# Decode attention on one core: where the first tile's value products stand in the TensorE queue

## Chip, cores, metric

The kernel runs on one core of one Trainium2 chip. The metric is device time in microseconds (us), the median of several executions. One execution of each kernel was also recorded by the profiler; all profile lines below come from such recordings, and their times count from the start of the span. On one core, a run more than 1.5% above the fastest of the same kernel counts as slow.

Some terms: tile *s* (0 to 7) is one step of the attention, eight heads of one batch row. *K0* to *K7* and *V0* to *V7* are the key and value tiles of the steps, 8.39 MB each. A tile has landed when the last of the sixteen landings that the trace records for its load has come. The granted clock is the share of TensorE's full clock that it was given in a stretch of time; TensorE is called warm at 1.00 and cold when it is clearly below.

## The reference, cut to what matters

```python
# A: attention of one query position over a cache; B=2, 32 heads, Sk=4096, Dh=128, D=512
q = (x @ wq).reshape(B, 1, 32, 128).transpose(0, 2, 1, 3)
p = softmax(einsum("bhqd,bhkd->bhqk", q, k_cache) * 128 ** -0.5)
a = einsum("bhqk,bhkd->bhqd", p, v_cache).transpose(...).reshape(B, 1, 4096) @ wo
# B: a small MLP, relu(x @ w1) @ w2;  g = sigmoid((x * gate_w).sum(-1))
return g * a + (1 - g) * b
```

There is one query per head, so every byte of K and V is read once: 134 of the 145 MB that are loaded.

## The kernel before

K has two buffers and V has one, 64 KB per partition each. The V buffer also holds the small weights at the start.

```python
kpool = ctx.enter_context(tc.tile_pool(name="kpool", bufs=2))
vpool = ctx.enter_context(tc.tile_pool(name="vpool", bufs=1))
# ... cut: PSUM pools, small tiles
```

The scores of a tile are made in four blocks. VectorE multiplies a block by the query in place (`mult`). TensorE adds up the products along the head dimension, with an identity matrix as weights (`red`); for block 1 it has no work, since VectorE adds that one up itself. VectorE then finishes the block (`scores`). The value products (`pv`, 64 matmuls) of a tile run during the next tile's step.

```python
for s in range(NS):
    if s >= 1: sums_mm(s - 1)
    mult(s, 0)                       # VectorE, needs K of tile s
    if s >= 2: evac(s - 2)
    if s >= 1: expand(s - 1)         # VectorE: probabilities for pv(s-1)
    red(s, 0)                        # TensorE
    if s == 0: mlp_h(); mlp_o()      # the MLP, TensorE (and a memset of hT on VectorE)
    # ... cut: comb, unpack, sums_inv of earlier tiles
    mult(s, 1)
    scores(s, 0)
    red(s, 1)                        # no TensorE work (block 1 is summed by VectorE)
    mult(s, 2)
    scores(s, 1)                     # VectorE, 8.7 us
    red(s, 2)                        # TensorE, waits for mult(s, 2)
    mult(s, 3)
    scores(s, 2)
    if s >= 1:
        pv(s - 1)                    # TensorE, the last reader of V of tile s-1
    red(s, 3)
    scores(s, 3)
    probs(s)
    if s == 0: load_v(0)
    if s + 2 < NS:
        load_k(s + 2)                # waits until K of tile s is free
        load_v(s + 1)                # waits until pv(s), in the next step, has read V of tile s
# ... cut: loads of V7 (into a K buffer) and wo, end of the last tile, output projection with wo
```

All these loads are issued by one queue (SyncE's, `SPq` in the profile), in program order. Each engine takes its own instructions in program order too; in the trace below, tile 0's value products have all their inputs at 80.9 us and start at 96.84 us, behind the sums that stand before them.

The softmax here doesn't subtract the row's maximum and nothing guards it: scores larger than these inputs give would overflow.

## Time and profile before

| | |
|---|---|
| time, median of 6 (20 with later runs) | 356.62 us (357.11) |
| the profiled execution | 355.56 us, span 353.9 us |
| mean DMA rate over the span | 411 GB/s |
| VectorE busy, TensorE busy | 74%, 52% |

The page cuts the span into 40 slices of 8.85 us. This is its row for the rate at which the DMA engines moved data, in GB/s:

```profile
GB/s 341 489 356 423 486 474 363 467 430 407 357 237 467 370 468 454 378 474 452 380 467 452 385 459 454 393 444 467 394 437 467 400 432 452 422 393 432 378 390 69
```

Between the start and the end, only the twelfth slice (97 to 106 us), at 237 GB/s, falls far below the others. The same place in a table of stretches; the columns are the stretch, its length, the busy time of PE (TensorE), PEld (its weight loads), DVE (VectorE), ACT and POOL, then granted TensorE clock, DMA share, GB/s:

```profile
90.00:96.50 6.50, 5.96 (x15) 2.18 (x15) 6.50 (x2) 0.00 (x0) 0.00 (x0) 0.53 0.77 333
96.50:101.80 5.30, 3.98 (x66) 1.70 (x65) 5.30 (x2) 0.00 (x0) 0.00 (x0) 1.00 0.42 139
101.80:108.00 6.20, 4.53 (x15) 1.75 (x15) 2.22 (x2) 0.00 (x0) 0.00 (x0) 0.72 0.93 391
...
135.00:137.00 2.00, 0.98 (x20) 0.36 (x13) 2.00 (x2) 0.00 (x0) 0.00 (x0) 1.00 1.18 500
```

The rates of such short stretches scatter (some read over 500). So I find holes from the packets themselves: a hole is where packets of fewer than 12 of the 16 DMA engines are under way. By that measure there is one after the start, 96.5 to 101.9 us (dips of under 0.5 us are left out here and below).

What did the queue wait for? The timeline of the loads' issues (start, length, issuing queue, line, operation, destination and source):

```profile
100.53 0.33 SPq L104 DMA_DIRECT2D vt<-in_A_v_cache_dram  x1
108.55 0.33 SPq L104 DMA_DIRECT2D kt<-in_A_k_cache_dram  x1
136.02 0.33 SPq L104 DMA_DIRECT2D vt<-in_A_v_cache_dram  x1
145.63 0.33 SPq L104 DMA_DIRECT2D kt<-in_A_k_cache_dram  x1
173.34 0.33 SPq L104 DMA_DIRECT2D vt<-in_A_v_cache_dram  x1
```

The first of them loads V1 into the buffer of V0. The TensorE timeline of that step (in brackets the idle time before a group, and what ended it):

```profile
78.80 5.30 PE L219 MATMUL red<-kt,ident 128*128 128x512 bf16 x16 [3.34 <-DVE kt L210]
90.54 6.37 PE L219 MATMUL red<-kt,ident 128*128 128x512 bf16 x16 [6.44 <-DVE kt L210]
96.84 3.64 PE L276 MATMUL o_ps<-vt,PT_sb 128*32 128x512 bf16 x64
103.47 5.04 PE L219 MATMUL red<-kt,ident 128*128 128x512 bf16 x16 [2.99 <-DVE kt L210]
```

L276 is `pv`. It frees the buffer at 100.5 us and the issue follows at once. TensorE sat idle for 6.44 us before the sums ahead of `pv`, waiting for a VectorE product that `pv` does not need.

The chain of waits, followed back from the end; four of its pieces (start, length, what):

```profile
255.28 42.59 DMA kt<-in_A_k_cache_dram
...
297.89 4.43 DVE kt L210
...
329.04 4.92 PE red L219 x16
...
345.67 5.29 PE a_ps L354 x24
```

The K7 load sits in the chain from its issue to its landing at 297.9 us, so the end of the kernel is tied to how far the stream has come. The rest, from 297.9 to 353.9, is work of VectorE and TensorE: 56.0 us, called the tail below.

### The profile page before, as it was taken

To read this page: it belongs to the slowest core of one execution; us is meant where nothing else is said; L and a number is where in the kernel's file an instruction comes from. 1 tells how busy PE (TensorE), PEld (TensorE's weight loads), DVE (VectorE), ACT (ScalarE), POOL (GpSimd) and SP (SyncE) were. 2 spreads that over 40 slices of the span, in tenths; PEclk is the share of its full clock that TensorE was granted. 3 is DMA by queue.
4 is the path that set the end of the run, shared out by engine and by line. 5 is a ranking of instruction groups with operands and counts; after the bars stand their busy time and mean duration, and the time that the engine had idled before them with its cause. 6 is when DMAs were issued, how large, how long until landed. Compare 5 with 4: busy or idle time off the path is not lost.

```text
span 353.9 us, 2493 instructions
## 1 busy us (share of the span) xinstructions
PE 184.8 (52%) x1091; PEld 74.6 (21%) x1091; DVE 262.3 (74%) x151; ACT 7.5 (2%) x23; POOL 6.1 (2%) x16
## 2 busy tenths in 40 slices
PE   0410856345764465564566286619424654728586
PEld 0100422111221122121222032203111221203232
DVE  3003189769977999599949994999569984999451
ACT  1000000000000000000000000000000000000000
POOL 6000000000000000000000000000000000000000
PEclk9985676688688869886976788687968698658889
DMA  8989998999869899899899899999999999999991
GB/s 341 489 356 423 486 474 363 467 430 407 357 237 467 370 468 454 378 474 452 380 467 452 385 459 454 393 444 467 394 437 467 400 432 452 422 393 432 378 390 69
DMA packets 4051, 145.60 MB, mean 411 GB/s; under 512 B 453, under 2 KB 586, under 8 KB 970
## 3 DMA queue, kind: packets, MB, share of 16 engines
q1 hardware_dynamic: 4036, 145.46, 95.9%
q8 instruction: 8, 0.13, 0.1%
q14 instruction: 1, 0.01, 0.0%
q10 hardware_dynamic: 6, 0.00, 0.0%
HBM read 145.46 MB, written 0.00 MB: 411 GB/s over the span
## 4 chain that ended last, share of the span: by engine, by line
DVE 59%; DMA 21%; PE 14%; issue 5%; ACT 0%; SPq 0%; DVEq 0%; ACTq 0%
DVE kt L210 32%; DMA kt<-in_A_k_cache_dram 21%; DVE sc L231 19%; PE red L219 10%; DVE PT_sb L251 4%; PE a_ps L354 2%; PE o_ps L276 2%; DVE osb L289 2%; DVE OT_sb L316 0%; DVE osb L287 0%; DVE tmp L307 0%; DVE rsg L268 0%; PE comb L301 0%; ACT e L237 0%; DVE rsg L267 0%
## 5 line engine op out<-in xcount | busy, mean ns | idle before, releaser
L219 PE MATMUL red<-kt,ident 128*128 128x512 bf16 x384 | 129.4, 512 | 139.8 <-DVE kt L210 139.8
L210 DVE TENSOR_TENSOR kt<-kt,qb 128x8192 bf16<-128x8192 bf16 x32 | 141.4, 4417 | 35.8 <-DMA kt<-in_A_k_cache_dram 26.9
L219 PEld LDWEIGHTS <-ident 128*128 128x128 bf16 x384 | 48.2, 125 | 217.6 <-issue 185.7
L231 DVE TENSOR_REDUCE sc<-kt 128x64 f32<-128x8192 bf16 x8 | 69.4, 8678 | 0.0
L231 DVE TENSOR_REDUCE sc<-red 128x64 f32<-128x512 f32 x24 | 16.5, 686 | 36.4 <-PE red L219 36.4
L276 PE MATMUL o_ps<-vt,PT_sb 128*32 128x512 bf16 x448 | 25.5, 380 | 0.0
L251 DVE TENSOR_TENSOR PT_sb<-e,tmask 128x2048 bf16<-128x2048 bf16 x8 | 18.3, 2283 | 0.6 <-ACT e L237 0.6
L276 PEld LDWEIGHTS <-PT_sb 128*32 128x32 bf16 x512 | 13.3, 100 | 18.0 <-issue 4.5
L237 ACT ACTIVATE e<-sc 128x256 bf16<-128x256 f32 x8 | 3.3, 417 | 285.6 <-DVE sc L231 285.6
L289 DVE SCALAR_TENSOR_TENSOR osb<-o_ps,jmask,osb 128x128 f32<-128x128 f32 x24 | 8.4, 351 | 0.8
L257 PE MATMUL gs<-partials,heads 128*128 128x1 f32 x16 | 3.0, 259 | 11.1 <-ACT e L237 11.1
L195 PE MATMUL mm<-vt 128*32 128x512 bf16 x64 | 5.7, 514 | 4.3 <-DMA vt<-in_A_wq_dram 3.7
L354 PE MATMUL a_ps<-kt,OT_sb 128*2 128x512 bf16 x32 | 7.2, 379 | 0.0
L276 PE MATMUL o_ps<-kt,PT_sb 128*32 128x512 bf16 x64 | 5.5, 508 | 1.9 <-DVE PT_sb L251 1.9
L307 DVE SCALAR_TENSOR_TENSOR tmp<-comb,rsg,umask 128x128 f32<-128x128 f32 x8 | 2.8, 346 | 4.2 <-PE comb L301 4.2
L257 PEld LDWEIGHTS gs<-partials,heads 128*128 128x128 f32 x16 | 2.4, 188 | 15.0 <-ACT e L237 13.2
L159 PE MATMUL comb<-ident,vt 2*128 2x2 bf16 (+1 forms) x8 | 0.6, 173 | 7.8 <-DMA vt<-in_gate_w_dram 5.6
L354 PE MATMUL a_ps<-vt,hT 128*2 128x512 bf16 x11 | 3.9, 524 | 0.5 <-ACT hT L347 0.5
L437 DVE CAST res<-a_ps 2x256 bf16<-2x256 f32 x1 | 0.4, 412 | 4.6 <-PE a_ps L354 4.6
L195 PEld LDWEIGHTS <-vt 128*32 128x32 bf16 x64 | 2.2, 119 | 7.4 <-issue 6.9
L354 PEld LDWEIGHTS <-OT_sb 128*2 128x2 bf16 x32 | 2.6, 84 | 4.1
L132 POOL TENSOR_SCALAR_AFFINE_SELECT vt<-vt 32x512 f32<-32x512 f32 x4 | 3.4, 847 | 0.2
(40 smaller groups left out, 33.1 us busy)
## 6 DMA issues: line engine op xcount, KB each, us to landing
vt<-in_A_wq_dram SPq DMA_DIRECT2D x1, 4096.0 KB, 12.1
kt<-in_A_v_cache_dram SPq DMA_DIRECT2D x1, 4096.0 KB, 31.3
kt<-in_A_v_cache_dram SPq DMA_DIRECT2D x2, 2048.0 KB, 40.2
kt<-in_A_wo_dram SPq DMA_DIRECT2D x3, 1024.0 KB, 9.5
vt<-in_B_w_dram SPq DMA_DIRECT2D x1, 1376.0 KB, 33.8
vt<-in_B_w_dram SPq DMA_DIRECT2D x1, 1280.0 KB, 36.5
kt<-in_A_wo_dram SPq DMA_DIRECT2D x1, 512.0 KB, 12.3
kt<-in_A_wo_dram SPq DMA_DIRECT2D x2, 256.0 KB, 11.6
```

Source lines behind the costliest of these rows:

```text
L132: nc.gpsimd.affine_select(out=sel[k * CG : (k + 1) * CG].rearrange("p j (t a) -> p j t a", t=T), in_=sel[k * CG : (k + 1) * CG].rearrange( ...
L195: nc.tensor.matmul(ps[j * CG : (j + 1) * CG, :], lhsT=xbp[:, b, c, e, :], rhs=wq_v[:, c, 2 * j + e, :, :], start=(c == 0 and e == 0), stop ...
L210: nc.vector.tensor_tensor(out=kt, in0=kt, in1=q, op=ALU.mult)
L219: nc.tensor.matmul(ps, lhsT=ident, rhs=prod[:, :, j * RW : (j + 1) * RW], start=(j == 0), stop=(j == Dh // RW - 1),)
L231: nc.vector.reduce_sum(out=sc_t[s][:, u * CU : (u + 1) * CU], in_=red_t.pop((s, u)), axis=AX.X)
L237: nc.scalar.activation(out=e, in_=sc_t.pop(s), func=ACT.Exp, scale=inv_sqrt_dh, accum_out=partials[:, s : s + 1],)
L251: nc.vector.tensor_tensor(out=out_, in0=e.to_broadcast(shape), in1=m.to_broadcast(shape), op=ALU.mult)
L257: nc.tensor.matmul(rs_t[s], lhsT=heads.rearrange("p t a -> p (t a)"), rhs=partials[:, s : s + 1], start=True, stop=True,)
L276: nc.tensor.matmul(o_t[s][k * CG : (k + 1) * CG, :], lhsT=PT_sb[:, s % 2, q, :], rhs=v_t[s][:, q * JB : (q + 1) * JB, :], start=(q < NCG), ...
L289: nc.vector.scalar_tensor_tensor(out=osb, in0=o[:, j, :], scalar=jmask[:, j : j + 1], in1=osb, op0=ALU.mult, op1=ALU.add,)
L307: nc.vector.scalar_tensor_tensor(out=tmp, in0=ps, scalar=rs_t.pop(s), in1=umask.unsqueeze(1).to_broadcast([P, DR, DA]), op0=ALU.mult, op1= ...
L354: nc.tensor.matmul(a_ps, lhsT=lhsT, rhs=rhs, start=start, stop=stop)
```

## The change

The value products of tile 0 are to run behind one score block of tile 1 instead of three, so that the V buffer is free sooner. Nothing else moves.

```diff
         scores(s, 0)
+        if s == 1:
+            pv(0)
         red(s, 1)
         mult(s, 2)
         scores(s, 1)
         red(s, 2)
         mult(s, 3)
         scores(s, 2)
-        if s >= 1:
+        if s >= 2:
             pv(s - 1)
         red(s, 3)
```

## The prediction

> **What bounds the kernel now.** Two resources are nearly even. The K/V stream: from 102 to 346 us the DMA queues run without a hole, and one 8.39 MB tile takes 19.35 us (spacing of tiles in the trace's packets), 433 GB/s, 38.7 us for a K and V pair. The Trainium skill, "DMA: Bandwidth & Descriptors", section "Where 436 GB/s comes from", puts the port ceiling at 435 GB/s; this trace agrees. VectorE: one tile step takes 37.1 us (spacing of successive tiles' first products in the timeline). So after the start the stream is the longer one, by 1.6 us a step, and the chain of waits shows it late: a 42.6 us DMA piece ends with the landing of the eighth K tile at 297.9 us; VectorE waits for K at 259.2 (3.22 us) and 297.9 (1.52 us). The tail follows the stream: the last output weights land at 348.9, span end 353.9.
>
> **The hole.** The packets show one hole after the start: 96.5 to 101.9 us, 5.4 us (the page's slice at 97 to 106 us shows 237 GB/s). Next comes the second V tile, into the single V buffer, which the first value products still read; they ran 96.84 to 100.5 us because the in-order TensorE puts them behind the third block's column sums (90.54 to 96.9), which wait for a VectorE product. The load was issued at 100.53.
>
> **What the change does.** No work is added or removed; 64 matmuls (3.64 us) move ahead of that sum. Their inputs are early: expanded probabilities at 80.9 us, V landed at about 79.5, the sums of block 0 end at 84.1. So they run 84.1 to about 88 us, before the third block's product is ready (90.5): that sum is not delayed. The V load is issued near 88, before the third K tile has drained (96.5): hole gone, V1 5.4 us earlier.
>
> **How much survives.** The next V load is issued at 136.02 us after the second tile's value products, which VectorE paces, plus 1.34 us from issue to first packet = 137.4. Today its data starts at 140.8; the shortened stream would want 135.4. So a new hole of about 2 us opens there and the carried shift is 140.8 - 137.4 = 3.4 us. The next V load has more slack (174.7 against 179.5), so 3.4 carries on. VectorE allows as much: its wait of 3.22 us at the seventh tile vanishes, the eighth's stays 1 to 2 us.
>
> Against it: "TensorE: Matmul & The Clock Gate", Part 1, says the default state is throttled and activity releases it; the trace agrees (granted clock 0.5 after idle stretches, 1.0 during the value products). These no longer warm TensorE before the second tile's last sums (5.04 us today; the first tile's cold ones took 5.72), for which VectorE waits. I take off 0.7 us as an estimate: it delays VectorE and the 136 us issue. Net 2.7 us.
>
> **Prediction: 353.8 us (-0.8%), range 352.0 to 355.8.** Faster by over 2%: 0.03; within 2%: 0.95; slower by over 2%: 0.02.
>
> **Right if the profile shows:** tile 0's value products at 84 to 88 us; second V load issued near 88; no hole at 96 to 102; a hole of 1.5 to 3 us near 135 to 138; seventh K tile landing near 256.4, VectorE waiting under 1 us for it; eighth near 295.1; output weights landing 2 to 3.5 us earlier; last sums of tile 1 taking 5.5 to 6 us.
>
> **Wrong if:** V lands after 84 us and TensorE stalls with the sums behind it; clock history delays tile 1's value products, widening the new hole; the hole of before varies between runs, so 5.4 us is not typical; or the tail absorbs the gain. If no new hole opened, the gain would reach 4 us at most, because VectorE then binds.

## The result, and the profile after

The median is **354.65 us** (10 runs, 349.5 to 357.34) against 357.11 us (20 runs of the kernel before, 355.15 to 359.4). A ratio is the mean time of one kernel's fast runs over the other's in the same rounds, so it is not quite the ratio of those medians: 0.9878, 95% interval 0.984 to 0.9917. That counts as the same within 2%, but the gain is clear of noise. One caution: a single execution at 349.5 us makes five of the ten runs "slow" by the 1.5% rule. With all runs of both, the means are 354.43 and 357.36, a ratio of 0.9918. Two later sets on other chips gave 0.9902 and 0.9946.

| profiled execution | before | after |
|---|---|---|
| time, span (us) | 355.56, 353.9 | 351.2, 349.5 |
| hole in the stream (us) | 96.5 to 101.9 | 135.1 to 136.4 |
| K6, K7 landed (us) | 259.2, 297.9 | 256.1, 294.8 |
| from K7's first product to the end (us) | 56.0 | 54.7 |

The same row of the page:

```profile
GB/s 319 514 368 407 514 368 473 428 413 474 375 465 480 368 466 377 360 480 428 414 473 368 473 398 452 465 375 465 459 398 458 390 459 465 390 405 424 404 391 66
```

The slice at 237 GB/s is gone. The same stretches as before:

```profile
90.00:96.50 6.50, 3.49 (x16) 1.46 (x15) 6.50 (x1) 0.00 (x0) 0.00 (x0) 1.00 0.98 423
96.50:101.80 5.30, 0.00 (x0) 0.00 (x0) 5.30 (x2) 0.00 (x0) 0.00 (x0) 0.70 1.09 470
101.80:108.00 6.20, 4.90 (x16) 1.77 (x15) 1.81 (x3) 0.00 (x0) 0.00 (x0) 0.71 0.83 359
...
135.00:137.00 2.00, 0.10 (x4) 0.10 (x1) 2.00 (x2) 0.00 (x0) 0.00 (x0) 1.00 1.27 434
```

The stretch of the old hole carries 470 in place of 139 GB/s. The new hole near 135 us is too short to stand out in a 2 us stretch; the packets show it (no new 64 KB packet of a load starts between 134.6 and 136.1 us). The issues:

```profile
87.03 0.33 SPq L104 DMA_DIRECT2D vt<-in_A_v_cache_dram  x1
107.74 0.33 SPq L104 DMA_DIRECT2D kt<-in_A_k_cache_dram  x1
135.15 0.33 SPq L104 DMA_DIRECT2D vt<-in_A_v_cache_dram  x1
144.82 0.33 SPq L104 DMA_DIRECT2D kt<-in_A_k_cache_dram  x1
172.46 0.33 SPq L104 DMA_DIRECT2D vt<-in_A_v_cache_dram  x1
```

The V1 load comes 13.5 us earlier. The later issues, up to that of K7 (255.28 and 254.38 us), come only 0.8 to 0.9 us earlier, because VectorE paces them. Most of that lead, 0.7 us, is there at the K2 load already (73.72 before, 73.05 after), ahead of the changed place: in this execution the sums and the MLP of tile 0 ran at a higher granted clock (0.62 against 0.57 from 33 to 43 us). The TensorE timeline:

```profile
78.14 5.29 PE L219 MATMUL red<-kt,ident 128*128 128x512 bf16 x16 [3.34 <-DVE kt L210]
83.35 3.64 PE L276 MATMUL o_ps<-vt,PT_sb 128*32 128x512 bf16 x64
89.88 3.61 PE L219 MATMUL red<-kt,ident 128*128 128x512 bf16 x16 [2.89 <-DVE kt L210]
102.81 4.90 PE L219 MATMUL red<-kt,ident 128*128 128x512 bf16 x16 [9.32 <-DVE kt L210]
```

The products fill the idle time. The sums behind them are not delayed, and run warm, in 3.61 instead of 6.37 us, which nobody needed. The chain:

```profile
254.38 40.40 DMA kt<-in_A_k_cache_dram
...
294.81 4.42 DVE kt L210
...
325.95 3.63 PE red L219 x16
...
341.30 5.29 PE a_ps L354 x24
```

Of the 4.4 us between the two spans, 3.1 us come from the stream (297.89 to 294.81). The other 1.3 us come from the last sums of tile 7: 4.92 us before (granted clock 0.73), 3.63 us after (1.00), for the same 16 matmuls.

### The profile page after: what moved, and what is told of

The parts are those of the page before. It is cut to its first block, busy times and chain, and to the rows that moved or that the text cites. A ratio compares the mean times of both kernels' runs of the same rounds, so it can differ in the third digit from the quotient of the medians.

```text
span 349.5 us, 2493 instructions
## 1 busy us (share of the span) xinstructions
PE 179.6 (51%) x1091; PEld 73.0 (21%) x1091; DVE 262.1 (75%) x151; ACT 7.5 (2%) x23; POOL 6.1 (2%) x16
## 4 chain that ended last, share of the span: by engine, by line
DVE 60%; DMA 20%; PE 13%; issue 5%; ACT 0%; SPq 0%; DVEq 0%; ACTq 0%
DVE kt L210 33%; DMA kt<-in_A_k_cache_dram 20%; DVE sc L231 20%; PE red L219 10%; DVE PT_sb L251 4%; PE a_ps L354 2%; PE o_ps L276 2%; DVE osb L289 2%; DVE OT_sb L316 0%; DVE tmp L307 0%; DVE osb L287 0%; DVE rsg L268 0%; PE comb L301 0%; ACT e L237 0%; DVE rsg L267 0%
## 5 line engine op out<-in xcount | busy, mean ns | idle before, releaser
L219 PE MATMUL red<-kt,ident 128*128 128x512 bf16 x384 | 125.7, 499 | 140.4 <-DVE kt L210 140.4
L219 PEld LDWEIGHTS <-ident 128*128 128x128 bf16 x384 | 47.0, 122 | 215.9 <-issue 185.1
L301 PEld LDWEIGHTS comb<-osb,pick 128*128 128x128 f32 x16 | 2.9, 190 | 2.1 <-issue 1.3
```

Source lines behind the costliest of these rows:

```text
L219: nc.tensor.matmul(ps, lhsT=ident, rhs=prod[:, :, j * RW : (j + 1) * RW], start=(j == 0), stop=(j == Dh // RW - 1),)
L301: nc.tensor.matmul(comb_t[s], lhsT=pick, rhs=osb_t.pop(s), start=True, stop=True)
```

## The experiments

Theory A is the prediction's: the gain comes from the V buffer, which is free sooner, so that the hole closes. Theory B: it comes from TensorE's order and clock. Theory C, tested by the fourth run: the hole is not a cause at all.

| kernel (label) | median us, runs | before, same rounds | ratio (95% interval) | hole, us | K7's first product | tail, us |
|---|---|---|---|---|---|---|
| before, first profile | 357.11, 20 | | | 96.5–101.9 | 297.9 | 56.0 |
| changed, first profile | 354.65, 10 | 357.11 | 0.9878 (0.984–0.9917) | 135.1–136.4 | 294.8 | 54.7 |
| e1_after_again | 354.79, 6 | 357.44 | 0.9902 (0.9863–0.9941) | 135.2–137.5 | 295.0 | 58.7 |
| e2_decouple | 354.07, 6 | 357.44 | 0.9906 (0.9882–0.9929) | 135.1–138.0 | 295.5 | 56.2 |
| e3_held | 364.88, 6 | 357.44 | 1.0219 (1.0188–1.025) | 96.3–110.3 | 306.6 | 58.8 |
| e4_pool_memset | 350.35, 6 | 357.44 | 0.982 (0.9786–0.9853) | none | 295.0 | 56.1 |
| e5_two_early | 352.31, 6 | 357.81 | 0.9848 (0.982–0.9876) | 173.8–175.5 | 294.8 | 56.3 |
| e6_all_early | 355.9, 6 | 357.81 | 0.9956 (0.993–0.9983) | 328.8–334.5 | 296.4 | 57.7 |
| e7_after_pool | 351.41, 6 | 357.81 | 0.9821 (0.9793–0.9849) | none | 292.2 | 57.4 |
| e8_pool_again | 350.08, 4 | 357.81 | 0.9787 (0.9762–0.9811) | none | 292.3 | 56.1 |
| e9_after_pair | 355.1, 6 | 356.7 | 0.9946 (0.9919–0.9973) | 135.0–138.2 | 295.7 | 56.2 |
| e10_two_pair | 351.61, 6 | 356.7 | 0.9877 (0.9838–0.9915) | 173.8–175.6 | 294.4 | 54.7 |

Hole, first product and tail are from each kernel's profiled execution; dips of up to 2.6 us after 329 us, where the last V load ends and the output weights begin, are told only for e6. By the 2% rule e3, e4, e7 and e8 count as unclear and the others as the same; every interval is clear of 1. e1 to e4, e5 to e8 and e9 with e10 share a chip each.

### e1_after_again: the changed kernel once more

> The changed kernel once more, on the chip of the next three. Theory A (the V buffer: the second V load is issued earlier and the hole in the K/V stream closes): second V load issued at 86 to 89 us, no hole near 96 us, a smaller hole of 1 to 2.5 us near 135 us, the seventh and eighth K tiles land 2.5 to 3.5 us earlier than in the kernel before; time 2 to 4.5 us shorter. The 1.3 us that the profiled run won beyond that, in the last column sums of the last tile, may or may not come back: it is a matter of the granted clock. Theory B (the gain comes from the order and the clock on TensorE itself: the sums of block 2 no longer run cold, the start was 0.7 us quicker): same time, but the gain sits in shorter column sums.

The V1 load was issued at 88.15 us, the hole was at 135.2 to 137.5 us, and K6 and K7 landed 3.0 and 2.9 us earlier than in the kernel before. The stream's gain came back. The tail's did not: the last sums took 6.5 us (granted clock 0.54) and the span was 353.7 us, with K7 at nearly the same time as in the first profile. One piece of its chain, against 3.63 us in the first profile of the same kernel:

```profile
326.13 6.52 PE red L219 x16
```

So of the profiled 4.4 us, the 3.1 us in the stream are the change's: e1 did not have the early lead (K2 was issued at 73.98 us) and still won 2.9 us there. The other 1.3 us are a higher clock that the first execution happened to get.

### e2_decouple: the old order, but nobody holds the buffer

```diff
-                rhs=v_t[s][:, q * JB : (q + 1) * JB, :],
+                rhs=(
+                    k_t[1][:, (q % (NQ // 2)) * JB : (q % (NQ // 2) + 1) * JB, :]
+                    if s == 0
+                    else v_t[s][:, q * JB : (q + 1) * JB, :]
+                ),
```

This is an edit of the kernel before. It computes wrong values; the comparison with the reference does not notice one tile's share of the output.

> Order of the kernel before on every engine, but the first tile's value products read the first half of the second K tile, so that nobody reads the first V tile and its buffer is free at once (wrong values on purpose). Theory A: the second V load is issued near 80 us, when the first V tile has landed; no hole near 96 us; hole of 1 to 2.5 us near 135 us; time within 1 us of the changed kernel's on this chip, although TensorE still does the value products behind the third block's sums. Theory B: TensorE's order is that of before, so time within 1 us of the kernel before.

The V1 load was issued at 79.36 us while `pv` ran at 95.2 us, in the old place:

```profile
79.36 0.33 SPq L104 DMA_DIRECT2D vt<-in_A_v_cache_dram  x1
...
95.23 3.64 PE L276 MATMUL o_ps<-kt,PT_sb 128*32 128x512 bf16 x64
```

The hole near 96 us was gone; the one near 135 us was 2.9 us long, a little over the expected 1 to 2.5. The time was 354.07 us, 0.7 us from the changed kernel on the same chip and 3.4 us below the kernel before. The gain therefore does not need TensorE's new order. Theory B falls.

### e3_held: the new order, but one matmul still holds the buffer

```diff
         if s == 1:
-            pv(0)
+            pv(0, 0, NQ - 1)
...
         red(s, 3)
+        if s == 1:
+            pv(0, NQ - 1, NQ)
         scores(s, 3)
```

This is an edit of the changed kernel.

> The changed kernel with 63 of the 64 first value products in the new place and the last one behind the fourth block's sums, so that the V buffer is held until about 108 us. Theory A: second V load issued near 108 us, a hole from 96.5 to about 109.7 us, 13 us in place of 5.4; time about 8 us longer than the kernel before (6 to 9). Theory B: TensorE's order is the changed kernel's but for one matmul, so the time is the changed kernel's within 1 us.

The V1 load was issued at 109.19 us, and the hole lasted from 96.3 to 110.3 us, 14 us.

```profile
109.19 0.33 SPq L104 DMA_DIRECT2D vt<-in_A_v_cache_dram  x1
```

The time rose by 7.4 us over the kernel before (364.88 against 357.44) and by 10 over the changed kernel. A hole 8.6 us longer cost 8.7 us at K7's first product (306.6 against 297.9): in this part of the stream a lost microsecond is a lost microsecond at K7.

### e4_pool_memset: close the hole from the other side

```diff
         if FREM:
-            nc.vector.memset(hT[: P - FREM, :, FF:], 0.0)
+            nc.gpsimd.memset(hT[: P - FREM, :, FF:], 0.0)
```

This is an edit of the kernel before; the value products stay where they were. The memset is 0.06 us of VectorE work. But VectorE is in order, and the memset has to wait for the MLP on TensorE and ScalarE, so the next product of tile 0 waited too. In the profile of the kernel before, that wait reads as 8.89 us of "issue".

> The kernel before, value products where they were; only the small memset of hT moves from VectorE to GpSimd, so that VectorE does not sit 8.9 us at 36.7 to 45.6 us behind the MLP. Theory A: VectorE's whole timeline up to the seventh tile comes about 8.5 us earlier, the old order issues the second V load near 92 us, before the stream drains at 96.5, and the third near 127.5: no hole at either place. The stream is 5.4 us ahead and the time 4.5 to 6 us shorter than before, more than the changed kernel gains. Theory C (VectorE and stream are bound elsewhere, the hole is no cause): VectorE only waits longer for the seventh and eighth K tiles, time within 1 us of before.

VectorE made its first two products back to back (32.43 to 41.2 us). Here is the second product of the kernel before, then the two of this run, then this run's V1 issue:

```profile
45.63 4.42 DVE L210 TENSOR_TENSOR kt<-kt,qb 128x8192 bf16<-128x8192 bf16 x1 [8.89 <-issue]
...
32.43 8.76 DVE L210 TENSOR_TENSOR kt<-kt,qb 128x8192 bf16<-128x8192 bf16 x2 [22.58 <-DMA kt<-in_A_k_cache_dram]
...
94.47 0.33 SPq L104 DMA_DIRECT2D vt<-in_A_v_cache_dram  x1
```

V1 was issued at 94.47 us and V2 at 130.07 us, both before the stream ran dry. No hole was left (only a dip of 0.4 us at 96.7 us). The time fell by 7.1 us, more than the expected 4.5 to 6. Theory C falls: the old place of the value products does no harm once VectorE comes earlier. K7, however, landed only at 295.0 us; e8 takes this up.

### e5_two_early: move the second tile's products too

```diff
-        if s == 1:
-            pv(0)
+        if s in (1, 2):
+            pv(s - 1)
...
-        if s >= 2:
+        if s >= 3:
             pv(s - 1)
```

This and the next are edits of the changed kernel.

> The changed kernel with the second tile's value products moved too (behind one score block of the third tile). Theory A: second V tile lands near 118 us, its products run at about 118 to 122 us, third V load issued near 122.5 in place of 135 to 136; the remaining hole near 135 us is gone; the K tiles from the fifth on land 1 to 2.5 us earlier than in the changed kernel. VectorE is then the limit at the seventh tile, so the time is only 0.5 to 1.5 us below the changed kernel's (353.5 on the last chip). If the second hole did not cost anything, the K tiles land when they did and the time is the same within 0.5 us.

The hole near 135 us went away (V2 issued at 123.5 us) and a third one opened at 173.8 to 175.5 us, where the next products, in the old place, hold the buffer until the V3 load at 174.37 us. I had expected the lead to last for the rest of the stream; it lasted one K tile. K4 landed 2.1 us earlier than in the first profile of the changed kernel, K7 at the same 294.8 us. The time was nevertheless shorter (see e10). (The "353.5 on the last chip" of the expectation is not a measured time: the changed kernel's median there was 354.79 us.)

### e6_all_early: move all of them

```diff
-        if s == 1:
-            pv(0)
+        if s >= 1:
+            pv(s - 1)
...
-        if s >= 2:
-            pv(s - 1)
```

> Every tile's value products behind one score block. Theory A: no hole anywhere, as in the run with two; from the fifth tile on the V tile lands only just before or after the sums of block 0 end, so TensorE waits up to 2 us for it, with 3 us or more to spare before VectorE needs the sums of block 2. Time that of the run with two moved, within 1 us. A rival, that value products early in the step hold up the sums, would make it 2 us or more slower.

Half a miss. The stream had no hole up to K7, which landed at 292.2 us, 5.7 us earlier than in the kernel before. But the time was 355.9 us, 3.6 us above the run with two. VectorE started K7 only at 296.43 us and did not wait for it: it had become the limit. Here is its wait for the fourth block's sums in tiles 5 and 6, in this kernel and then in the kernel before (VectorE timeline):

```profile
258.30 0.69 DVE L231 TENSOR_REDUCE sc<-red 128x64 f32<-128x512 f32 x1 [5.21 <-PE red L219]
...
295.82 0.69 DVE L231 TENSOR_REDUCE sc<-red 128x64 f32<-128x512 f32 x1 [5.24 <-PE red L219]
```

```profile
255.29 0.69 DVE L231 TENSOR_REDUCE sc<-red 128x64 f32<-128x512 f32 x1 [3.10 <-PE red L219]
...
295.68 0.69 DVE L231 TENSOR_REDUCE sc<-red 128x64 f32<-128x512 f32 x1 [4.79 <-PE red L219]
```

Over tiles 2 to 6 these waits add up to 25.6 us, against 22.3 us before: 3.3 us more. In the old place, `pv` runs just before those sums; in the new one, TensorE has been idle. The granted clock over the sums of tiles 5 and 6 was 0.62 in both here, against 1.00 and 0.68 before, and the same 16 matmuls took 5.72 and 5.75 us, against 3.61 and 5.30. So a lower clock goes with the longer waits; that the idle time caused it is not shown, since no run varied the clock alone. The expectation named a rival, value products that hold up the sums behind them, and its number (2 us or more slower) came true. But VectorE never waited for the sums right behind them, those of the third block; it waited for the fourth block's. TensorE itself waited longer for V tiles than expected (4.0 us in tile 6, up to 2 expected), which cost VectorE nothing.

### e7_after_pool and e8_pool_again: do the two gains add?

e7 is the changed kernel with e4's one-line edit; e8 is e4's kernel again, on e7's chip.

> The changed kernel with the small memset of hT on GpSimd instead of VectorE. Theory A: with VectorE 8 us earlier the old order had no hole left (none was in the run with that memset alone), so moving the value products adds nothing on top: the time is that of the memset alone within 1 us (350.4 on the last chip). If the two gains had different causes they would add, and the time would be near 347.5.

> The memset alone once more, as the partner of the run before on the same chip: 350 us, 6 to 7 us below the kernel before, no hole at 96 or 135 us. Its first profile showed the eighth K tile at 295.0 us, no earlier than in the changed kernel, although the first of the 16 landings came 2.4 us earlier than there; if that lag of the last landing was a matter of that one execution, this profile shows the tile at 292 to 294 us.

They do not add: 351.41 and 350.08 us, with ratios of 0.9821 and 0.9787 whose intervals overlap, and K7's first product at 292.2 us in e7 and 292.3 in e8. The 1.3 us between the medians are a little over the expected 1 us, and e7 is the slower one, far from the 347.5 us of gains that add. K7 landed at 292.2 us in e6, e7 and e8 alike, 5.7 us earlier than in the kernel before: that is what a stream without a hole gives here, however the hole is closed. In e8 the V1 load was issued at 91.93 us. Its K7 landed at 292.2 us, where e4's profile had 295.0. In e4's execution the sixteen landings of each late load were spread over some 4.1 us, against 1.9 us in e8's; the work waits for the last of them. What put part of the DMA engines behind in that execution stays open.

### e9_after_pair and e10_two_pair: the changed kernel and e5's, on one chip

> The changed kernel, partner of the next run on one chip. The stream theory: first product of the eighth tile at 294.5 to 295.5 us (294.8 and 295.0 so far); from there to the end of the span 54.7 to 58.8 us, which differs from run to run with the granted clock in the last sums and products. Time 354.5 us, 2.5 to 3.5 us below before.

> Two tiles' value products moved, on the same chip as the changed kernel. In its first profile a third hole at 173.8 to 175.5 us gave the second move's gain back: first product of the eighth tile at 294.8 us, the same as in the changed kernel, yet the timed runs were some 2 us shorter, on another chip. If that difference was chip or chance, the two are now within 1 us. If it is real (1.5 to 2.5 us shorter again), it is either in the stream (eighth tile's first product under 294 us in this profile) or behind it, in the tail.

The difference is real: 355.1 against 351.61 us, 3.5 us, more than the 1.5 to 2.5 us allowed for. e9 itself missed its expectations narrowly: 1.6 us below the kernel before (2.5 to 3.5 expected) and K7's first product at 295.67 us (294.5 to 295.5). The two profiled executions differ by 2.7 us: 1.3 us lie in the stream (295.67 against 294.41 us) and 1.5 us in the tail (56.2 against 54.7 us). e9's own hole was 3.2 us long, because VectorE waited 5.99 us for the last sums of tile 1 (4.39 us in the first profile of the same kernel) and the V2 load came at 136.98 us. e5's kernel does not have that hole, so a cold phase there cannot lengthen it. Its shorter tail lies in the first 48 value products of tile 7: 2.77 us at a granted clock of 1.00, against 4.26 us at 0.63 in e9. Whether the second move brings that about or this execution happened to get it is open; tails of 54.7 to 58.8 us have been seen with the same work. So is the rest of the 3.5 us, which the profiled pair does not show.

## Why the prediction was right or wrong

- **Cause and mechanism: right, and shown.** The predicted 353.8 us with a range of 352.0 to 355.8 holds the measured 354.65. The gain follows the time at which the V buffer is free (e2, e3), not the order on TensorE, and the move brings nothing more once the hole is closed otherwise (e7 against e8).
- **Value products and issue: right.** They ran at 83.35 to 87.0 us (84 to 88 predicted), and the V1 load was issued at 87.03 (near 88).
- **The new hole near 135 to 138 us: right, size variable.** It was 1.3, 2.3 and 3.2 us long in three profiles of the changed kernel; 1.5 to 3 was predicted. It is the main reason that 5.4 us of hole bought about 3. One term in it was too large: 1.34 us from a load's issue to its first packet. The packets show 0.95 us, at the old hole (100.53 to 101.48) as at the new one (135.15 to 136.10); 1.35 us is the time until 12 of the 16 engines were at work again (101.88). The Trainium skill, "DMA: Bandwidth & Descriptors", section "Latency and other measured facts", gives some 0.6 us to the first byte on this path; counted from the end of the 0.33 us issue record, this trace agrees (0.62 us). A cost was left out: the first sixteen 64 KB packets after a hole took 3.0 to 3.2 us on average in seven profiles, against 2.42 us within the stream, so by my estimate a hole costs 0.6 to 0.8 us more than its length. The old hole paid this too, so only closing it for good saves it: K7 came 5.7 us earlier in e7, for 5.4 us of hole.
- **Net shift of the stream: right, with compensating errors.** 2.7 us was predicted; K7's first product came 3.1, 2.9 and 2.2 us earlier in the three profiles. The sum took off 0.4 us too much for the first packet and 0.7 us for a colder clock that the first profile did not have, and left out both the slow first packets and the spread of a load's landings (2.6 us for K7 in the first profile, 2.0 before). It was also lucky there with the V2 load, 0.9 us early, of which 0.7 us came from the start.
- **The clock term: mis-sized.** The prediction charged 0.7 us to colder last sums in tile 1 ("5.5 to 6 us"). They took 4.90 us in the profiled execution. VectorE's wait for them was 4.39, 4.58 and 5.99 us in three executions of the changed kernel, and 4.53 (before), 5.96 (e2), 4.74 (e4) and 6.05 (e8) with the products in their old place. The wait depends on the execution, not on the move. The Trainium skill, "TensorE: Matmul & The Clock Gate", Part 1, describes a clock that rises with sustained activity and falls in idle time; the trace agrees (granted 0.53 around tile 1's third-block sums before, after 6.44 us of idle time, and 1.00 after the change, close behind the value products), but which phase an execution is in cannot be read off the change.
- **VectorE's wait for K6 under 1 us: missed by a hair** (1.02 us; no wait in e1, 2.40 us in e9). **Output weights 2 to 3.5 us earlier: wrong in the first profile**, which had 5.3 us (348.9 to 343.6); e1 had 3.4 and e9 1.1. The tail adds its own clock phase to the stream's shift, which the prediction left out.
- **"If no new hole opened, at most 4 us, because VectorE then binds": half right.** e6 has no hole near 135 us, shows VectorE binding and gained 1.9 us by medians. With two tiles moved the gain was 5.5 and 5.1 us, of which the profiles show 3.1 and 3.5 in the stream. With VectorE relieved in tile 0 (e4, e8) it was 7.1 and 7.7 us, of which e8's profile shows 5.6 in the stream. One reason that the profiles show less than the medians: the profiled execution of the kernel before (355.56 us) was itself 1.6 us below its median.

## What to carry to other kernels

When two streams are within a few per cent of each other, look for the one transfer whose buffer is held by work standing in an in-order queue behind something it does not need, and compare the time of its issue with the time at which the transfer before it ends. Before banking a closed hole, do that sum for the next transfers too: the smallest slack among them (here the V2 load, then V3) caps the gain. And look further up for what makes the pacing engine late: a 0.06 us memset on the wrong engine cost more than the placement, and moving it to GpSimd alone, with everything else as in the kernel before, gave the fastest kernel (350.1 to 350.4 us).

## What the Trainium skill lacked or had wrong

- "DMA: Bandwidth & Descriptors", section "Where 436 GB/s comes from", says that for transfers between HBM and SBUF the HBM side, some 358 GB/s, binds. Here, with one core at work, HBM to SBUF loads ran at 433 GB/s for over 200 us (8.39 MB per 19.35 us), at the port ceiling that the same section gives. The section lacks the condition that stands under "Measured (HBM→SBUF, 128 partitions, SWDGE, issued from GpSimd)" on the same page: some 358 GB/s is each core's part when both cores of the HBM domain stream.
- No page that I read tells how far the sixteen landings of one load can drift apart. In these profiles the spread for an 8.39 MB K tile was from 0.4 us (K0 in e8) up to 4.2 us (K6 in e4), and the work waits for the last.
- No page that I read tells what restarting an idle stream costs: the first sixteen 64 KB packets after a hole took 3.0 to 3.2 us on average, against 2.42 us within the stream.
- "TensorE: Matmul & The Clock Gate", Part 1, says that the clock's window runs freely, so that one kernel's warm-up differs from run to run, and puts the loss at under 1% of a typical span. Here the differences went on to the end of the kernel and were larger: the same 16 sums of tile 7 took 3.63 and 6.52 us in two executions of the changed kernel (granted clock 1.00 and 0.54), and their tails were 54.7 and 58.7 us, 1.1% of the time, as much as the change itself.
